# Batch 3's reciprocals sent through DMA, its last scores a group earlier: joining a pipeline's prologue to its steady pattern

## The chip, the cores and the metric

The kernel runs on 1 core of one Trainium2 chip. The metric is the device time in microseconds (us), where lower is better. Executions of the kernel before agree within about 0.3%, so runs are compared by the median and by a ratio. That ratio is the mean time of one kernel's fast runs over the mean time of the other's fast runs of the same rounds, with a 95% interval; it is not quite the quotient of the medians quoted here. The time before is 366.54 us. "Span" is the length of the one execution that the profiler recorded; it is a little shorter than the time (364.9 us for the kernel before).

## The reference

Eight batches of 576 tokens pass through sliding-window attention (window 128, a slope per head), and the 4608 tokens that come out pass through a gated FFN:

```python
scores = scale * np.matmul(q, k.transpose(0, 1, 3, 2))      # q, k, v: 8 x 8 heads x 576 x 64
scores = np.where(mask, scores + bias[None], -1000000000.0) # mask: 0 <= distance < 128
attn = np.exp(scores - max); attn = attn / attn.sum(axis=-1)
x = np.matmul(attn, v)                                      # then to (4608, 512)
out = (gelu(x @ w_gate) * (x @ w_val)) @ w_out              # 512 -> 1536 -> 512
```

## The kernel before

The FFN goes in nine groups of 512 tokens. Each group has an FFN part (12 gate/value blocks) and an output part (eight "halves", two for each tile of 128 tokens). The attention of later batches is woven between these, so that TensorE (PE) always has matmuls while ScalarE (ACT) does the exps and VectorE (DVE) the masks. A batch goes through five steps:

- q and k are transposed by DMA (`transposes_dma`, on the SP queue),
- scores, exps and mask (`scores2` for one block column, `scores` for the two parts s = 0, 1),
- row sums on PE and a reciprocal on DVE (`sums`),
- the spread of the reciprocals over all partitions, either by a small matmul (`spread_pe`) or through DRAM (`spread_dma`),
- values, multiplied by the spread reciprocal (`values`).

```python
def transposes_dma(b):                       # SP queue
    for src, dst in ((ks, kT), (qs, qT)):
        nc.sync.dma_start_transpose(out=dst[b % 2]..., in_=src[b % 2]...)

def spread_dma(b):                           # SP queue, behind whatever stands there
    d = d_pool.tile([4, 2, S], FP32, name="rd")
    nc.sync.dma_start(out=d..., in_=sumrow[b][0:128:16, :])           # rd <- r
    for i in (0, 1):
        nc.sync.dma_start(out=recip[b][64 * i:64 * i + 64, :, :],     # rb <- rd
                          in_=d[:, i, :].unsqueeze(0).to_broadcast((64, 4, S)))

def spread_pe(b, s):                         # four small matmuls into four banks
    ...                                      # and four copies on ACT and DVE
# ... cut ...
2: [("s", 3, 1, (0, 1), lambda: sums(3, 0)), 0, ("s", 3, 1, (2, 3)), 1,
    ("spread", 3, 0), ("pv", 3, 0), ("s2", 4), ("sum", 3, 1), 2,
    ("s", 4, 0, (0, 1)), 3, ("spread", 3, 1), ("pv", 3, 1), 4, ("s", 4, 0, (2, 3)), 5,
    ("s", 4, 1, (0, 1)), 6, 7, ("s", 4, 1, (2, 3))],
# ... cut ...
for g in range(NG):
    for b in ((), (2, 3), (4,))[g] if g < 3 else ():
        transposes_dma(b)
    if g + 2 < B:
        load_v(g + 2)                        # Pool queue: waits until vb's old batch is used up
    for f in range(3 if g == 0 else 0, NF):
        gate_val(g, f)
        # ... cut ...
        if 3 <= g < B - 1:                   # the steady pattern
            if f == 0:
                sums(g + 1, 0); sums(g + 1, 1)
                spread_dma(g + 1)
                if g + 2 < B:
                    transposes_dma(g + 2)
            elif f in (8, 10):
                for s in (0, 1):
                    values(g + 1, s, (f - 8, f - 7))
    if g + 3 < B:
        load_qk(g + 3)                       # Pool queue, behind load_v
    for item in steps(g):                    # output halves, scores and the rest, in order
        ...
```

The list for group 2 is written by hand: an integer is an output half, "s2" and "s" are scores, "sum" sums, "spread" the spread by PE, "pv" values. From group 3 on, every group has the same steady pattern.

The softmax here doesn't subtract the row's maximum and nothing guards it: scores larger than these inputs give would overflow.

## Time and profile before

| what | value |
|---|---|
| time, median of 3 | 366.54 us |
| profiled span | 364.9 us |
| PE busy | 351.6 us, 96% |
| share of PE in the chain that ended last | 86% |

The stretches view gives, for a window of time, the busy time of each engine (with the number of instructions in brackets), then the granted TensorE clock as a share of full speed, the DMA share and GB/s. For groups 2, 3 and 4 of the kernel before:

```profile
111.20:151.40 40.20, 39.73 (x325) 19.17 (x329) 24.55 (x39) 24.96 (x47) 17.81 (x23) 1.00 1.31 116
151.40:189.50 38.10, 37.41 (x285) 18.01 (x290) 22.18 (x33) 22.46 (x40) 16.62 (x20) 1.00 1.47 158
189.50:226.90 37.40, 37.14 (x285) 17.88 (x288) 20.88 (x32) 20.92 (x36) 4.19 (x5) 1.00 0.76 125
```

The third number is PE's busy time: it fills its group in all three, at full clock. Group 2 takes 40.2 us, group 3 38.1 and the fully steady group 4 37.4. So there is something to gain in groups 2 and 3, but only the few microseconds above 37.4, less the work that group 2 has beyond a steady group.

### The profile page before, as it was taken

The numbers are of one execution on the slowest core, as the hardware profiler recorded it, in microseconds if no ns is written. First come the engines' busy times: TensorE is split into PE (matmuls) and PEld (weight loads), VectorE is DVE, ScalarE is ACT, GpSimd is POOL, SyncE is SP. The second block draws the span as 40 slices with busy tenths as digits, with TensorE's granted clock in tenths as the row PEclk, the third lists the DMA queues.
The fourth block names the chain that finished last, engine by engine and source line by source line (L and its number), as shares of the span: only waits on it lengthen the run. The fifth ranks groups of instructions, "written<-read, shape, count | busy, mean of one in ns | idle before, by whom it ended". The sixth has DMA issues, their size and how long they took to land.

```text
span 364.9 us, 6652 instructions
## 1 busy us (share of the span) xinstructions
PE 351.6 (96%) x2638; PEld 170.7 (47%) x2682; DVE 189.0 (52%) x307; ACT 187.2 (51%) x339; POOL 108.1 (30%) x140
## 2 busy tenths in 40 slices
PE   8889999999999999999999999999999999999995
PEld 3455545444454445444444444444444444444442
DVE  4794448533795469474547554745564404302320
ACT  5953487435966376933783278436842223323321
POOL 8945859923519203900940040000000000000000
PEclk9999999999999999999999999999999999999999
DMA  9999999999999994999991992092206030011002
GB/s 105 133 202 180 171 160 183 178 152 194 140 150 98 147 105 81 147 106 224 116 202 53 224 91 89 32 216 58 88 31 131 0 115 2 0 60 58 0 31 86
DMA packets 151168, 41.41 MB, mean 113 GB/s; under 512 B 138816, under 2 KB 144448, under 8 KB 151136
## 3 DMA queue, kind: packets, MB, share of 16 engines
q0 software_dynamic: 112608, 18.88, 67.9%
q1 hardware_dynamic: 38528, 22.10, 28.4%
q8 instruction: 21, 0.34, 0.4%
q14 instruction: 11, 0.09, 0.1%
HBM read 42.47 MB, written 9.51 MB: 142 GB/s over the span
## 4 chain that ended last, share of the span: by engine, by line
PE 86%; ACT 8%; DVE 2%; issue 1%; POOL 1%; POOLq 0%; ACTq 0%; DVEq 0%
PE ps L292 50%; PE ps L308 23%; ACT P L181 6%; PE ps L273 4%; PE ps L174 4%; PE ps L232 2%; PE ps L255 1%; DVE xT L279 1%; DVE P L184 1%; ACT L181 1%; ACT emask L359 1%; PE ps L153 1%; DVE r L241 0%; POOL ks L115 0%; ACT osb L313 0%
## 5 line engine op out<-in xcount | busy, mean ns | idle before, releaser
L297 DVE TENSOR_TENSOR hT<-ps,gelu 128x512 bf16<-128x512 f32 (+2 forms) x111 | 74.4, 674 | 121.8 <-PE ps L292 107.1
L296 ACT ACTIVATE gelu<-ps 128x512 bf16<-128x512 f32 (+2 forms) x111 | 64.9, 586 | 120.0 <-PE ps L292 119.8
L292 PE MATMUL ps<-xT,wg 128*128 128x512 bf16 (+2 forms) x430 | 111.0, 373 | 1.7 <-DVE xT L279 0.7
L292 PE MATMUL ps<-xT,wv 128*128 128x512 bf16 (+2 forms) x435 | 110.4, 373 | 0.6
L308 PE MATMUL ps<-wo,hT 128*128 128x512 bf16 x413 | 97.2, 380 | 1.5 <-issue 0.8
L181 ACT ACTIVATE P<-ps 128x512 bf16<-128x512 f32 x144 | 74.3, 629 | 6.9 <-PE ps L174 6.8
L292 PEld LDWEIGHTS <-wv 128*128 128x128 bf16 x444 | 43.3, 98 | 50.5 <-issue 0.5
L292 PEld LDWEIGHTS <-wg 128*128 128x128 bf16 x444 | 41.9, 98 | 49.8 <-issue 2.3
L184 DVE TENSOR_TENSOR P<-P,emask 128x1024 bf16<-128x1024 bf16 x72 | 48.3, 685 | 31.2 <-ACT P L181 30.9
L308 PEld LDWEIGHTS <-hT 128*128 128x128 bf16 x432 | 39.7, 98 | 49.0 <-issue 4.4
L95 POOL DMA_DIRECT2D vb<-in_v_dram x40 | 33.7, 867 | 71.1 <-PE ps L273 70.4
L313 ACT COPY osb<-ps 128x512 f32<-128x512 f32 x36 | 21.7, 602 | 37.2 <-PE ps L308 32.8
L95 POOL DMA_DIRECT2D qs<-in_q_dram x35 | 29.7, 878 | 25.5 <-DMA qT<-qs 12.9
L95 POOL DMA_DIRECT2D ks<-in_k_dram x35 | 29.6, 882 | 9.6 <-DMA qs<-in_q_dram 6.6
L241 DVE RECIPROCAL r<-ps 128x320 f32<-128x320 f32 (+1 forms) x16 | 30.7, 1938 | 2.6 <-PE ps L232 2.6
L174 PE MATMUL ps<-qT,kT 64*128 64x256 bf16 (+1 forms) x384 | 23.5, 245 | 2.2 <-ACT kT L147 0.6
L279 DVE TENSOR_TENSOR xT<-ps,rb 128x320 bf16<-128x320 f32 (+1 forms) x64 | 24.7, 448 | 0.5 <-DMA rb<-rd 0.5
L174 PEld LDWEIGHTS <-kT 64*128 64x128 bf16 x384 | 12.9, 94 | 17.2 <-issue 12.7
L273 PE MATMUL ps<-P,vb 128*64 128x128 bf16 (+2 forms) x384 | 18.4, 243 | 0.1
L273 PEld LDWEIGHTS <-vb 128*64 128x64 bf16 x384 | 14.7, 110 | 6.8 <-issue 6.8
L232 PE MATMUL ps<-P,ones 128*32 128x128 bf16 (+2 forms) x384 | 10.8, 243 | 1.3 <-DVE P L184 1.1
L232 PEld LDWEIGHTS <-ones 128*32 128x32 bf16 x384 | 7.9, 96 | 5.5 <-issue 4.7
(50 smaller groups left out, 98.7 us busy)
## 6 DMA issues: line engine op xcount, KB each, us to landing
out_dram<-osb SPq DMA_DIRECT2D x36, 256.0 KB, 2.3
rb<-rd SPq DMA_DIRECT2D x8, 576.0 KB, 7.4
vb<-in_v_dram POOLq DMA_DIRECT2D x32, 128.0 KB, 5.7
qs<-in_q_dram POOLq DMA_DIRECT2D x28, 128.0 KB, 6.9
ks<-in_k_dram POOLq DMA_DIRECT2D x28, 128.0 KB, 6.3
wg<-in_moe_w_gate_dram POOLq DMA_DIRECT2D x4, 384.0 KB, 10.7
wv<-in_moe_w_val_dram POOLq DMA_DIRECT2D x4, 384.0 KB, 11.9
wo<-in_moe_w_out_dram POOLq DMA_DIRECT2D x2, 768.0 KB, 11.3
```

The lines of the kernel that those rows point to most:

```text
L95: nc.gpsimd.dma_start(out=t[lo:128, j, :].rearrange("p (h d) -> p h d", h=H), in_=src[b][:, 128 * j - 64 + lo:128 * j + 64, :].rearrange(" ...
L174: nc.tensor.matmul(out=ps[:, col:col + 128 * n].rearrange("p (n t) -> p n t", n=n), lhsT=blocks(kT, b, i, c, j, 1).rearrange("p n t -> p ( ...
L181: nc.scalar.activation(out=dst, in_=src, func=AF.Exp, scale=0.125)
L184: nc.vector.tensor_tensor(out=dst, in0=dst, in1=m, op=ALU.mult)
L232: nc.tensor.matmul(out=ps[32 * c:32 * c + 32, a:e], lhsT=ones[:, min(j, 1), i, :], rhs=prob(b, s, c, i, j, e - a), start=(i == 0 and j == ...
L241: nc.vector.reciprocal(sumrow[b][:, lo:hi], ps[:, 0:hi - lo])
L273: nc.tensor.matmul(out=ps[64 * i:64 * i + 64, a:e], lhsT=vb[b % 2][:, j, 64 * h:64 * h + 64], rhs=prob(b, s, c, i, j, e - a), start=(j == ...
L279: nc.vector.tensor_tensor(out=xT[:, c, b * S + lo:b * S + hi], in0=ps[:, 0:hi - lo], in1=recip[b][:, c, lo:hi], op=ALU.mult)
L292: nc.tensor.matmul(out=ps[:, 0:hi - lo], lhsT=w[:, c, 128 * f:128 * (f + 1)], rhs=xT[:, c, t0 + lo:t0 + hi], start=(c == 0), stop=(c == 3))
L296: nc.scalar.activation(out=gl[:, 0:hi - lo], in_=pg[:, 0:hi - lo], func=AF.Gelu)
L297: nc.vector.tensor_tensor(out=hid[g][:, f, lo:hi], in0=pv[:, 0:hi - lo], in1=gl[:, 0:hi - lo], op=ALU.mult)
L308: nc.tensor.matmul(out=po, lhsT=hid[g][:, f, 128 * t:128 * (t + 1)], rhs=wo[:, f, :], start=(f == 0), stop=(f == NF - 1))
```

## The change

The intent is to start the steady pattern one group earlier. The last scores of batch 3 move from group 2 to the end of group 1. Sums of batch 3 then come beside FFN blocks 0 and 1 of group 2; its reciprocals are spread through DMA and no longer by PE matmuls; its values come half at the 12th FFN block and half among the output halves. The transposes of batch 4, which stood first in group 2, now stand behind the spread on the SP queue, as they do in every steady group.

```diff
         1: [ ... cut ...
-            ("spread", 2, 1), ("pv", 2, 1), ("s", 3, 0, (2, 3)), 7],
-        2: [("s", 3, 1, (0, 1), lambda: sums(3, 0)), 0, ("s", 3, 1, (2, 3)), 1,
-            ("spread", 3, 0), ("pv", 3, 0), ("s2", 4), ("sum", 3, 1), 2,
-            ("s", 4, 0, (0, 1)), 3, ("spread", 3, 1), ("pv", 3, 1), 4, ("s", 4, 0, (2, 3)), 5,
-            ("s", 4, 1, (0, 1)), 6, 7, ("s", 4, 1, (2, 3))],
+            ("spread", 2, 1), ("pv", 2, 1), ("s", 3, 0, (2, 3)), 7, ("s", 3, 1, (0, 1)),
+            ("s", 3, 1, (2, 3))],
+        2: [("s2", 4), ("s", 4, 0, (0, 1)), 0, 1, ("s", 4, 0, (2, 3)), 2,
+            ("pv", 3, 0, (2, 3)), 3, ("s", 4, 1, (0, 1)), 4, ("pv", 3, 1, (2, 3)), 5,
+            ("s", 4, 1, (2, 3)), 6, 7],
# ... cut ...
-        for b in ((), (2, 3), (4,))[g] if g < 3 else ():
+        for b in ((), (2, 3))[g] if g < 2 else ():
             transposes_dma(b)
# ... cut ...
-            if 3 <= g < B - 1:
+            if 2 <= g < B - 1:
                 if f == 0:
                     sums(g + 1, 0)
+                if f == (1 if g == 2 else 0):
                     sums(g + 1, 1)
                     spread_dma(g + 1)
                     if g + 2 < B:
                         transposes_dma(g + 2)
-                elif f in (8, 10):
+                elif f in ((8, 10) if g > 2 else (11,)):
                     for s in (0, 1):
-                        values(g + 1, s, (f - 8, f - 7))
+                        values(g + 1, s, (0, 1) if f != 10 else (2, 3))
```

More of the change, by code (lines that the diff above doesn't have):

```diff
@@ L440 @@
     RUN = {"s2": scores2, "s": scores, "sum": sums, "spread": spread_pe,
-           "pv": lambda b, s: values(b, s, range(4))}
+           "pv": lambda b, s, cs=range(4): values(b, s, cs)}
     for g in range(NG):
-        for b in ((), (2, 3), (4,))[g] if g < 3 else ():
+        for b in ((), (2, 3))[g] if g < 2 else ():
             transposes_dma(b)
```

## The prediction

> **What bounds the kernel now.** I read the page first: the busy times, then the chain that ended last by engine.
>
> ```profile
> PE 351.6 (96%) x2638; PEld 170.7 (47%) x2682; DVE 189.0 (52%) x307; ACT 187.2 (51%) x339; POOL 108.1 (30%) x140
> PE 86%; ACT 8%; DVE 2%; issue 1%; POOL 1%; POOLq 0%; ACTq 0%; DVEq 0%
> ```
>
> TensorE (PE) is busy 96% of the 364.9 us span and carries 86% of the chain, so the time changes only by matmuls that leave PE and by gaps in which PE waits. Next I read the chain in order of time over groups 2 and 3, the stretch that the change touches.
>
> ```profile
> 131.97 0.61 PE ps L174 x12
> ...
> 136.54 0.75 PE ps L255 x8
> 137.29 1.11 PE ps L273 x24
> ...
> 142.63 0.66 PE ps L255 x8
> 143.29 1.00 PE ps L273 x24
> ...
> 150.88 0.56 PE ps L174 x12
> 151.45 2.08 ACT P L181 x4
> 153.55 0.70 DVE P L184
> 154.30 0.60 PE ps L232 x21
> ```
>
> L174 is scores, L232 sums, L255 the spread of the reciprocals by PE, L273 values, L292 gate and value products, L308 the output product. From the PE timeline, group 2 runs from 111.2 to 151.4 and group 3 from 151.45 to 189.5. Group 4, in full steady pattern, takes 189.52 to 226.91 = 37.4 us, group 3 takes 38.1: the last three lines of the fence show why. Its sums wait for the exps and the mask of scores issued at 150.88, the last thing of group 2. That is 0.65 us over a steady group.
>
> The third view is the timeline of the SP queue, which issues spread and transposes in one order. This is group 3:
>
> ```profile
> 159.86 0.71 SPq L245 DMA_DIRECT2D rd<-r  x1
> 161.74 1.32 SPq L247 DMA_DIRECT2D rb<-rd  x2
> 163.29 6.85 SPq L167 DMA_TRANSPOSE kT<-ks  x1
> 170.31 3.10 SPq L167 DMA_TRANSPOSE qT<-qs  x1
> ```
>
> and this, in the DMA view of 170 to 176 us, is the last of them, with the time from issue to landing at the end:
>
> ```profile
> qT<-qs SPq DMA_TRANSPOSE x1, 4.9
> ```
>
> So from the end of the last reciprocal (159.83 on the DVE timeline) to q transposed in place is 170.31 + 4.9 - 159.83 = 15.4 us. The same sum gives 206.50 + 6.5 - 196.5 = 16.5 in group 4 and 244.09 + 5.3 - 233.9 = 15.5 in group 5. The scores that read it start at 176.26, 213.72 and 251.12, only 1.1, 0.7 and 1.7 us after the landings. The steady pattern hides this DMA chain, but with almost nothing to spare.
>
> **What the Trainium skill says.** "TensorE: Matmul & The Clock Gate", Part 3 (The mechanism): matmuls at different row groups of the array overlap. The trace agrees: the eight instructions of a spread take 0.66 to 0.75 us together, although one of them lasts 453 ns on average. So removing a spread is worth far less than its busy durations suggest. "DMA: Bandwidth & Descriptors", Anatomy of one DMA: about 2 us of a transfer is fixed, mostly completion. The trace agrees: 1.88 us pass between issuing the 18 KB rd and issuing rb, which waits for it. "ScalarE: Activation LUTs", What ACT_TABLE_LOAD costs: 1283 ns of load plus a drain, 2.66 us together. The trace shows the 1.28 us load and the next gelu 0.01 us behind it (112.26 and 113.55), so I count 1.28. The first page's Part 1: an idle PE falls to half clock after about a 3.4 us window; here the granted clock is 1.00 from 361 to 364 us and 0.57 from 364 to 365, so it falls at about 364.1, some 3 us after the last matmul ended at 361.1.
>
> **The change, part by part.**
>
> *Removed.* Both spreads of batch 3: 0.75 + 0.66 = 1.41 us of PE, all on the chain. Some 0.3 us of issue gaps between the many pieces of group 2 may go as well (the chain has 0.15 us at 131.82 and 0.16 us at 135.14). Four ACT and four DVE copies of about 0.44 us leave too, off the chain.
>
> *Moved out of group 3's way.* Group 2 now ends like a steady group, with two output tiles after the last scores. So the mask wait at the head of group 3 goes: -0.65 us.
>
> *Moved without cost of their own.* Sums (1.05 us, 48 matmuls) and values of batch 3 only change place. The last scores of batch 3 (24 matmuls, 1.09 us) go from group 2 to the end of group 1.
>
> *The new end of group 1.* Now two score calls follow output tile 7 with nothing between. I worked through ACT: exps of the earlier scores end at 111.76, the copy of tile 7 at 112.24 (both as now), then eight exps take 4.03 us (the run of eight at 133.12) to 116.15, the table load to 117.43, the first gelu to 118.05. PSUM has eight banks in rotation: the second half of the last score call needs tile 7's bank, free at 112.24, and the first gate product needs the bank of the first new exp, free at about 112.75. PE would reach that point at 112.3 (111.2 + 1.09), so it loses about 0.45 us. Group 2 starts at 112.78.
>
> *The reciprocals.* DVE takes them in program order: first product by 118.7, reciprocal 0 (about 2.1 us) by 120.8, second product by 121.4, reciprocal 1 (1.7) by 123.05. In steady groups the second reciprocal ends 7.0 us after the group starts (196.5 - 189.52); here it is 10.3, because ACT is behind and the second sum waits until gate block 1.
>
> *The DMA chain.* The reciprocals now go through rd and rb, and the transposes of batch 4 stand behind them on SP. Before, these were issued at 112.83, free of any reciprocal. Last reciprocal at 123.05 + 15.5 us (median of the three) = 138.55 until q of batch 4 is transposed.
>
> *Who needs it.* The first score call of batch 4 is now the very first item after the FFN of group 2. PE reaches it at 112.78 + 1.73 (gate 0) + 0.53 (sums) + 1.73 (gate 1) + 0.53 (sums) + 17.27 (ten gates of 1.727) + 0.1 (issue) + 1.06 (values beside block 11) = 135.7. **It waits 138.55 - 135.7 = 2.85 us.**
>
> *The sum.* Scores start at 138.6. A steady group needs 213.72 to 226.91 = 13.2 us from there, plus the two half values, 1.06 us: group 3 starts at about 152.9, against 151.45 now, +1.45. Group 3 then saves 0.65. Net +0.8 us; groups 4 to 8 repeat the same pattern. 366.54 + 0.8 = 367.3. I choose **367.4** because what is uncertain lies more on the slow side.
>
> **Rivals.**
>
> *The wait doesn't appear.* For it: the q and k loads of batch 5 (Pool, 112.08 to 125.1, slowed now by the transposes of batch 4) would run uncontended, and a wait needs 2.85 us of my arithmetic to hold. Against it: all three steady instances take over 15 us, and only 12.65 us lie between reciprocal and use. Without the wait the time is 366.54 - 1.41 - 0.3 - 0.65 + 0.45 = about 364.6.
>
> *The DMA chain is slower than in steady groups.* When transposes and loads ran together now, k and q took from 112.83 to 126.79 to issue, 14.0 us, against 10.1 us in group 3. If the loads of batch 5 overlap rd and rb by some us, the wait grows to 4 us, and the time to about 368.5. For it: DMA is at 9 tenths in this stretch. Against it: with the transposes away, the loads should be over near 125.7, by the run of loads issued back to back from 147 to 155.4.
>
> *The clock falls.* A gap near 3 us is where the clock fell at the end of the run. If it falls in the wait, the next 3.4 us run at half speed: about +1.7 us, to 369. I give it 1 in 5.
>
> *A later echo.* Values of batch 3 end some 4 us later than now, and the loads of v 5 and of q and k 6 wait for them; they would run into rb of group 3, where the slack was 1.1 us. The reciprocals there come no sooner, so I expect under 0.5 us.
>
> *ACT becomes the bound at the start of group 2.* It is 4 us behind, but eight banks let PE run on: the banks that gates 3 to 6 need come free at 118.7, 120.8, 121.5 and 123.9, which is before PE asks, except at gate 4, where the two are about even.
>
> **Range and chances.** From "no wait" (364.6) to "wait with a fallen clock" (369 to 370); the middle eight tenths are 365.2 to 369.6. A 2% step is 7.3 us: a gain of that size would need five times the work removed, a loss would need a wait of 9 us. Faster 0.01, within 0.97, slower 0.02.
>
> **What would show it.** In the changed trace: no L255 instruction after about 109; a gap of about 0.45 us on PE just before group 2; the rd issue at about 123; a PE gap of 2 to 4 us before L174 at 136 to 139, put down to a transpose (it may be named otherwise, since its releaser is a DMA); sums at the head of group 3 without a wait; group 3 in 37.4 us. It is wrong if q of batch 4 lands before 136, if the reciprocals end by 120, or if PE stalls at gates 3 to 6 for banks.

## The result, and the profile after

The changed kernel takes 371.48 us (370.96 to 372.10, 4 runs), where the kernel before took 366.65 us in the same rounds. The ratio to the kernel before is 1.0132, interval 1.0114 to 1.0149: 1.3% slower, where 0.2% was predicted, and above the predicted range. Executions over 1.5% slower than the fastest of the same kernel are left out of the means. The profiled span is 369.4 us against 364.9.

The page of the changed kernel, the lines that answer to those shown of before, and the row of the granted clock (40 slices of the span, in tenths):

```profile
PE 353.0 (96%) x2622; PEld 170.8 (46%) x2666; DVE 187.5 (51%) x303; ACT 186.0 (50%) x335; POOL 108.0 (29%) x140
PEclk9999999999999996999999999999999999999999
PE 84%; ACT 7%; DMA 3%; DVE 2%; issue 2%; POOL 1%; SPq 0%; POOLq 0%; ACTq 0%; DVEq 0%
```

By its records PE has 16 matmuls fewer, yet is busy 1.4 us longer. DMA appears in the chain with 3%, which it did not before. And in one slice the clock is down.

The stretches of groups 2, 3 and 4 of the changed kernel:

```profile
112.60:156.24 43.64, 40.10 (x283) 18.72 (x288) 23.17 (x35) 23.78 (x43) 13.61 (x18) 0.92 1.04 123
156.24:194.20 37.96, 37.31 (x284) 18.02 (x289) 21.04 (x32) 20.92 (x36) 19.25 (x23) 1.00 1.65 169
194.20:231.60 37.40, 37.14 (x285) 17.88 (x288) 20.89 (x32) 20.92 (x36) 4.18 (x5) 1.00 0.74 123
```

Group 3 starts at 156.24 in place of 151.4, 4.8 us later. Of these, 1.4 us lie at the end of group 1, where the moved scores now stand, and 3.4 us in group 2, although that group holds less work. Group 3 itself gains only 0.14 us. From group 4 on all is as before. So the loss that has to be explained lies in group 2, and the first place to look is its SP queue (start, time on the queue, line, kind, names). Before, the transposes of batch 4 stood alone there:

```profile
112.83 6.05 SPq L167 DMA_TRANSPOSE kT<-ks  x1
119.05 7.74 SPq L167 DMA_TRANSPOSE qT<-qs  x1
```

In the changed kernel they stand behind the spread:

```profile
122.97 0.71 SPq L245 DMA_DIRECT2D rd<-r  x1
124.98 1.32 SPq L247 DMA_DIRECT2D rb<-rd  x2
126.53 7.33 SPq L167 DMA_TRANSPOSE kT<-ks  x1
134.03 3.35 SPq L167 DMA_TRANSPOSE qT<-qs  x1
```

The same stretch in the chain in order of time, and then on PE, where the bracket at the end of a line is the idle time before it and what ended it:

```profile
134.03 4.86 DMA qT<-qs
138.89 0.14 issue
139.02 1.47 PE ps L174 x16
```

```profile
134.85 1.13 PE L273 MATMUL ps<-P,vb 128*64 128x192 bf16 x24
139.02 1.47 PE L174 MATMUL ps<-qT,kT 64*128 64x128 bf16 x16 [3.04 <-DMA qT<-qs]
140.42 0.61 PE L308 MATMUL ps<-wo,hT 128*128 128x512 bf16 x1
141.25 4.08 PE L308 MATMUL ps<-wo,hT 128*128 128x512 bf16 x10 [0.22 <-issue]
```

The last reciprocal ends at 122.9, rd is issued at once, q of batch 4 lands at 138.89, and PE has nothing to do from 135.98 to 139.02. This is the predicted wait. What follows it is the surprise: 16 score matmuls take 1.47 us where a steady group has 0.77, and ten output matmuls 4.08 us where twelve of a steady group take 2.70. The stretches view of the changed kernel shows why:

```profile
136.00:138.00 2.00, 0.00 (x0) 0.00 (x0) 1.18 (x4) 0.00 (x0) 0.00 (x0) 0.99 1.24 269
138.00:139.00 1.00, 0.00 (x0) 0.01 (x1) 0.00 (x0) 0.00 (x0) 0.00 (x0) 0.50 0.37 70
143.00:145.00 2.00, 2.00 (x7) 0.72 (x5) 0.41 (x1) 0.00 (x0) 0.00 (x0) 0.55 0.00 0
145.00:147.00 2.00, 2.00 (x16) 0.81 (x14) 0.03 (x1) 1.64 (x4) 0.00 (x0) 1.00 0.09 34
```

The clock goes to half at 138 and comes back at 144.8; the clock record of the trace has 137.96 and 6.83 us. Of these, 5.77 us lie after the restart at 139.02, so the slow clock costs half of that, 2.9 us.

### The profile page after: what moved, and what is told of

It is laid out like the page before. It is cut to its first block, busy times and chain, and to the rows that moved or that the text cites. A ratio compares the mean times of both kernels' runs of the same rounds, so it can differ in the third digit from the quotient of the medians.

```text
span 369.4 us, 6613 instructions
## 1 busy us (share of the span) xinstructions
PE 353.0 (96%) x2622; PEld 170.8 (46%) x2666; DVE 187.5 (51%) x303; ACT 186.0 (50%) x335; POOL 108.0 (29%) x140
## 4 chain that ended last, share of the span: by engine, by line
PE 84%; ACT 7%; DMA 3%; DVE 2%; issue 2%; POOL 1%; SPq 0%; POOLq 0%; ACTq 0%; DVEq 0%
PE ps L292 49%; PE ps L308 23%; ACT P L181 5%; PE ps L174 4%; PE ps L273 3%; DMA qT<-qs 3%; PE ps L232 2%; DVE xT L279 1%; PE ps L255 1%; ACT L181 1%; ACT emask L359 1%; DVE P L184 1%; PE ps L70 1%; PE ps L153 1%; DVE r L241 0%
## 5 line engine op out<-in xcount | busy, mean ns | idle before, releaser
L308 PE MATMUL ps<-wo,hT 128*128 128x512 bf16 x414 | 99.3, 385 | 1.5 <-issue 0.9
L174 PEld LDWEIGHTS <-kT 64*128 64x128 bf16 x384 | 13.4, 96 | 19.5 <-issue 15.3
## 6 DMA issues: line engine op xcount, KB each, us to landing
wo<-in_moe_w_out_dram POOLq DMA_DIRECT2D x2, 768.0 KB, 10.1
```

Of the source, the lines that this page charges most:

```text
L174: nc.tensor.matmul(out=ps[:, col:col + 128 * n].rearrange("p (n t) -> p n t", n=n), lhsT=blocks(kT, b, i, c, j, 1).rearrange("p n t -> p ( ...
L308: nc.tensor.matmul(out=po, lhsT=hid[g][:, f, 128 * t:128 * (t + 1)], rhs=wo[:, f, :], start=(f == 0), stop=(f == NF - 1))
```

## The experiments

The theory is: (a) PE waits because the transposes of batch 4 stand behind the reciprocals and the spread on one queue; (b) the wait makes the clock fall, which costs nearly as much again; (c) the late values of batch 3 delay loads, which then slow the spread of group 3, an echo. The rivals are that the new places of the scores, sums and values cost by themselves, or that ACT, 4 us behind at the start of group 2, is the bound. All outputs are right. Each ratio and each time before is of the same rounds, on one chip; runs of different experiments can come from different chips.

### 1. One part alone: the moved scores

```diff
 kernel before
-  ("spread", 2, 1), ("pv", 2, 1), ("s", 3, 0, (2, 3)), 7],
-  2: [("s", 3, 1, (0, 1), lambda: sums(3, 0)), 0, ("s", 3, 1, (2, 3)), 1,
+  ("spread", 2, 1), ("pv", 2, 1), ("s", 3, 0, (2, 3)), 7, ("s", 3, 1, (0, 1)), ("s", 3, 1, (2, 3))],
+  2: [("sum", 3, 0), 0, 1,
```

> The kernel before with one part of the change alone: the last scores of batch 3 move to the end of group 1, the spread stays on PE and the transposes stay first. Theory (this part costs only the short waits for ACT at the end of group 1, about 0.45 us, less the issue gaps that it removes): 366.65 + 0.2, within 0.6 us of the kernel before. Rival (ACT, 4 us behind at the start of group 2, is what made the changed kernel slow): over 369.

Measured: 367.95 us against 367.25, ratio 1.0019 (1.0002 to 1.0035): 0.7 us slower, a little more than the 0.6 us allowed for. The rival falls: the back-to-back scores and the ACT that is behind cost under 1 us.

### 2. One part undone: the transposes first

```diff
 changed kernel
-    for b in ((), (2, 3))[g] if g < 2 else ():
+    for b in ((), (2, 3), (4,))[g] if g < 3 else ():
         transposes_dma(b)
@@ behind spread_dma(g + 1)
-                    if g + 2 < B:
+                    if 4 < g + 2 < B:
                         transposes_dma(g + 2)
```

> The changed kernel with one part undone: the transposes of batch 4 issued at the start of group 2, ahead of the spread of batch 3, as before. Theory (PE waits because the transposes stand behind the reciprocals on the SP queue): q of batch 4 lands by about 128, the gap before its first scores and the clock fall are gone, time about 371.5 - 3.0 - 2.8 = 365.7 or a little less, though rd can't be issued before about 127 and the values of batch 3 may then wait for rb until 137. Rival (the new end of group 1 with its back-to-back scores costs the time, or the values at block 11): the time stays within 1 us of 371.5.

Measured: 374.32 us against 367.25, ratio 1.0188 (1.0149 to 1.0226). It is slower still, so my expectation was wrong. Its SP queue, and the line of DVE that multiplies the first values:

```profile
118.90 7.96 SPq L167 DMA_TRANSPOSE qT<-qs  x1
126.95 0.71 SPq L245 DMA_DIRECT2D rd<-r  x1
133.56 1.31 SPq L247 DMA_DIRECT2D rb<-rd  x2
```

```profile
141.33 1.55 DVE L279 TENSOR_TENSOR xT<-ps,rb 128x320 bf16<-128x320 f32 x4 [5.61 <-DMA rb<-rd]
```

Now q is in place in time and rb is late. The 18 KB of rd, issued behind the transposes while the loads of batch 5 also run, take 6.6 us from issue to the issue of rb, which waits for them (126.95 to 133.56), against 2.0 us in the changed kernel. DVE waits 5.61 us for rb, PE's banks stay full, and PE waits 5.34 us. The clock, which was expected to stay, falls in this wait too (3.41 us from 141.69 on). So the order on the queue is not the cause alone: the spread and the transposes together, with the loads around them, are too long for the order of work that this version has behind the FFN, and undoing the order on the queue only chooses which of the two is late. The Trainium skill has a possible reason why a small transfer can take so long, "DMA: Bandwidth & Descriptors", Queues, rings and completion order: each DMA engine takes the queue rows it has work for in turn, a whole packet at a time. The 6.6 us agree with that, but no run here shows single turns.

### 3. The whole DMA chain undone: the spread back on PE

```diff
 changed kernel, with the transposes first as in 2
-                    spread_dma(g + 1)
-                    if g + 2 < B:
-                        transposes_dma(g + 2)
+                    if g > 2:
+                        spread_dma(g + 1)
+                        if g + 2 < B:
+                            transposes_dma(g + 2)
+                elif g == 2 and f in (5, 6):
+                    spread_pe(3, f - 5)
```

> The changed kernel with the spread of batch 3 back on PE (beside FFN blocks 5 and 6) and the transposes of batch 4 first again, so no reciprocal goes through DMA in group 2; scores, sums, values and the order of the rest stay as changed. Theory (all of the loss is the DMA chain rd, rb, transposes, and the clock fall it causes): no gap before the first scores of batch 4, no clock fall, 1.41 us of spread matmuls back, ratio to the kernel before about 1.000 and a spread between runs under 1 us. Rival (the new places of scores, sums and values cost by themselves): ratio over 1.006.

Measured: 368.13 us against 366.75, ratio 1.0027 (1.0009 to 1.0046). In group 2 the gap and the clock fall are gone. But the ratio is not 1.000, the runs spread over 2.0 us, and the profile has a wait in a place where I had not expected one of this size, at the first scores of group 3:

```profile
159.74 0.71 SPq L245 DMA_DIRECT2D rd<-r  x1
163.48 1.32 SPq L247 DMA_DIRECT2D rb<-rd  x2
```

```profile
178.63 0.83 PE L174 MATMUL ps<-qT,kT 64*128 64x128 bf16 x16 [1.70 <-DMA qT<-qs]
```

rd to rb takes 3.74 us here against 1.88 in group 3 of the kernel before. This is the echo, and it is the subject of the next two runs.

### 4. The echo taken away

```diff
 changed kernel (loads_swapped), and the kernel of 3 (pe_back_swapped)
+        if g == 3:
+            load_qk(6)
         if g + 2 < B:
             load_v(g + 2)
@@ after the FFN part
-        if g + 3 < B:
+        if g != 3 and g + 3 < B:
             load_qk(g + 3)
```

The load of v of batch 5 overwrites the buffer of batch 3, so it waits for the last values of batch 3. In the changed kernel that is 151.94 us (its second part on the Pool queue), where it was 144.43. The loads of q and k of batch 6 stand behind it.

> The changed kernel with the loads of q and k of batch 6 queued ahead of the load of v of batch 5, so that they need not wait for the values of batch 3 and are over before group 3's reciprocals. Theory of an echo (these loads run into rd and rb of group 3): in group 3 the time from issuing rd to issuing rb falls from 3.97 to about 1.9 us, the wait of DVE for rb (1.69 us) and of PE for q of batch 5 (0.34) go, time 0.3 to 0.6 us lower, about 371. The wait in group 2 stays at 3 us. Rival (rd is slow in group 3 for another reason): 3.97 stays.

> The version with the spread of batch 3 back on PE, with the loads of q, k 6 queued ahead of the load of v 5 as well. In that version group 3 took 39.15 us against 37.4 of a steady group, and rd to rb 3.74 us. Theory (the echo, late loads that run into rd and rb of group 3, is worth 1.75 us there): rd to rb falls to about 1.9 us, group 3 to 37.4, span from 367.3 to about 365.5, ratio about 0.998. Rival (group 3 is slow there for another reason): ratio stays at 1.003.

Measured: pe_back_swapped 367.10 us against 367.18, ratio 0.9999 (0.9983 to 1.0015), and four runs within 0.5 us. rd to rb is 1.87 us:

```profile
159.79 0.71 SPq L245 DMA_DIRECT2D rd<-r  x1
161.66 1.32 SPq L247 DMA_DIRECT2D rb<-rd  x2
```

Group 3 takes 37.4 us in it, against 39.15. The span goes from 367.3 to 365.6, so the echo was 1.7 us in the profiled execution of that version. In times the difference is smaller and not clear: the ratios, 1.0027 and 0.9999, are of two chips, and their intervals overlap. This run also gave the 1.000 that run 3 had been expected to give.

loads_swapped: 371.37 us against 366.75, ratio 1.0120 (1.0099 to 1.0142). Its rd to rb in group 3 fell from 3.97 to 1.81 us, and its group 3 from 37.96 to 37.4 us, as expected. In the changed kernel the echo is thus worth 0.55 us in the profiled execution. In times, its ratio can't be told apart from the 1.0132 of the changed kernel. Its four times go with the granted clock: 369.95 us at 0.999, 370.76 at 0.995, 371.98 and 372.11 at 0.991.

### 5. The clock kept up in the wait

```diff
 changed kernel
-        2: [("s2", 4), ("s", 4, 0, (0, 1)), ...
+        2: [("busy", 12), ("s2", 4), ("s", 4, 0, (0, 1)), ...    # warm6: 6 in place of 12
@@
-    RUN = {"s2": scores2, ...
+    RUN = {"busy": keep_busy, "s2": scores2, ...
```

`keep_busy(n)` is the kernel's own helper: the next bank first receives n matmuls of zeros, which the scores then overwrite.

> The changed kernel with twelve matmuls of zeros (0.22 us each, 2.6 us) put into the wait before the first scores of batch 4, where PE stood idle 3.04 us and the granted clock then fell to 0.50 from about 138 to 145. Theory (the wait itself costs 3.0 us and the clock fall it causes another 2.8): the landing of q of batch 4 stays at 138.9 us, the clock stays at 1.00, the rest of group 2 takes 14.3 us in place of 17.3, time about 371.5 - 2.8 = 368.7. Rival (the loss after the wait comes from the new order of products and values itself, the clock is only a sign of it): time stays at 371.5 or rises.

> The changed kernel with six zero matmuls (1.3 us) at the start of its wait, half of those of the earlier run: they shorten the idle stretch from 3.0 to about 1.7 us but do not fill it. Theory (the clock falls after about 2 to 3 us of idle PE, whatever else is in the order): no fall, clock 0.999 to 1.000, the wait ends when it did, same time as with twelve, ratio about 1.006. Rival (only a filled gap keeps the clock): clock 0.991 to 0.995, ratio as the changed kernel. A third outcome, both levels in different runs, would mean that the fall depends on where a free-running window stands.

> A repeat of the run with twelve zero matmuls, whose four times spread over 4.8 us (368.51 to 373.29) although three of them had a clock of 1.000. Theory (the DMA chain's own length varies from run to run): median 1.5 to 3 us below the unaltered changed kernel of the same chip, spread again over 1.5 us. Rival (the first set was disturbed): four times within 0.7 us, ratio about 1.006.

> The changed kernel unaltered, on the same chip as the two runs with zero matmuls, as their base. Expected: ratio to the kernel before 1.011 to 1.015, granted clock 0.991 or 0.995 in nearly every run.

| run | median | four times | ratio (interval) |
|---|---|---|---|
| warm12 | 370.06 | 368.51, 370.93, 373.29, 369.19 | 1.0091 (1.0038 to 1.0144) |
| after_again | 370.64 | 370.71, 375.55, 369.84, 370.56 | 1.0083 (1.0056 to 1.0109) |
| warm6 | 369.83 | 369.17, 372.16, 368.67, 370.49 | 1.0080 (1.0039 to 1.0122) |
| warm12_again | 370.00 | 370.64, 368.51, 372.62, 369.35 | 1.0085 (1.0038 to 1.0132) |

The 375.55 of after_again does not enter its ratio; the median of its three fast runs is 370.56 us. That ratio, 1.0083, lies below the 1.011 to 1.015 that were expected, and its interval does not meet that of the same kernel's first measurement (1.0114 to 1.0149). So the ratio of one kernel can differ by 0.5% from one set of rounds to another, and ratios of different sets can't be compared more closely than that.

In the profiled executions the theory holds: in none of the three warm runs does the clock fall near the wait, and from the first scores of batch 4 to group 3 the chain has 14.65 us in each of them, against 17.4 in the changed kernel and 16.3 in after_again, whose fall lasts 3.41 us. For warm6 this is shown for that one execution only. Its four granted clocks are 0.994, 0.995, 1.000 and 0.995, not the 0.999 to 1.000 that were expected; the 0.994 is a fall at 11.34 us, in the start-up, and where the falls of the two runs at 0.995 lie is not known.

And the times don't show the gain. Medians of warm runs and of the unaltered kernel lie within 1 us, and the expected 1.5 to 3 us are missing. The profile of warm12_again shows one reason, again at the first scores of group 3:

```profile
180.41 0.84 PE L174 MATMUL ps<-qT,kT 64*128 64x128 bf16 x16 [1.89 <-DMA qT<-qs]
```

Here the echo costs 1.9 us, while the profiled executions of warm12 and warm6 have no wait at that place. So the echo differs from one execution to the next, and it can hide the clock. That called for one more pair, in which the echo is taken out of both.

### 6. The clock alone

The edit of warm12 on loads_swapped, beside loads_swapped itself, five rounds each on the same chip.

> The changed kernel without the echo in group 3, as base for the next run on the same chip. Expected: ratio to the kernel before near 1.012, runs at the granted clocks 0.991, 0.995 or 0.999, slower the lower the clock.

> The changed kernel with twelve zero matmuls in its wait and without the echo in group 3 (loads of q, k 6 ahead of v 5): the clock fall alone is taken from loads_swapped_again. Theory (the fall costs 1.7 or 2.85 us in each execution, and only the echo, 0 to 2 us, hid this in the times of the earlier runs): times lie 1.5 to 3 us below loads_swapped_again, within 1 us of each other, near 368.7, ratio about 1.005. Rival (the fall costs little in executions that aren't profiled): both ratios within 0.002.

Measured: loads_swapped_again 370.77 us, ratio 1.0100 (1.0080 to 1.0120), granted clock 0.995 in five runs and 0.991 in one. warm12_swapped 368.69 us, ratio 1.0044 (1.0031 to 1.0057), clock 0.998 to 1.000, six runs within 0.5 us. The two intervals don't touch. The first scores of batch 4 in the two profiles, loads_swapped_again first:

```profile
140.83 1.47 PE L174 MATMUL ps<-qT,kT 64*128 64x128 bf16 x16 [3.46 <-DMA qT<-qs]
139.88 0.84 PE L174 MATMUL ps<-qT,kT 64*128 64x128 bf16 x16 [0.64 <-DMA qT<-qs]
```

With the wait filled, 2.1 us of time are gone, and with the echo gone too, so is the wide scatter of the warm runs. Not all of the 2.1 us can be put down to the clock: a granted clock of 0.995, which five of the six runs of loads_swapped_again have, amounts to one fall of 3.41 us, and such a fall costs at most half of that, 1.7 us; in the two profiles the chain from these scores to group 3 goes from 16.1 to 14.65 us, 1.45 us. The remaining 0.4 us or more are not explained.

### 7. The dose of the wait

```diff
 changed kernel
-                if f == (1 if g == 2 else 0):
+                if f == (4 if g == 2 else 0):
                     sums(g + 1, 1)
```

> The changed kernel with the second sums, and so the whole DMA chain behind them, at FFN block 4 in place of 1: the last reciprocal ends some 2.7 us later (at about 125.6). Theory (the wait is set one to one by the end of the last reciprocal plus the chain): q of batch 4 lands about 2.7 us later, the gap grows from 3.0 to 5.7 us, the clock fall stays one fall, time about 371.5 + 2.7 = 374.2. Rival (the chain is held up by something else, such as the loads of batch 5, so that the start hardly matters): landing and time within 0.8 us of the changed kernel's.

Measured: 372.06 us (median of its three fast runs; the fourth, 377.11, is slow) against 366.75, ratio 1.0136 (1.0121 to 1.0152). The last reciprocal ends 2.0 us later (124.95 against 122.95), not the 2.7 I had worked out. q lands 1.3 us later, and the gap is longer:

```profile
140.37 0.83 PE L174 MATMUL ps<-qT,kT 64*128 64x128 bf16 x16 [4.18 <-DMA qT<-qs]
```

So the wait follows the reciprocals, though not one to one, for the chain behind them took 15.3 us in place of 15.9. The time did not follow, and the 374.2 us that were expected did not come: in the profiled execution the clock fall lasted 3.41 us and not 6.83, which gives back about what the longer wait took. Where the clock falls has to be read before a time is put down to a wait.

### 8. Two orders that cover the wait

```diff
 values_first: changed kernel, only the list of group 2
-        2: [("s2", 4), ("s", 4, 0, (0, 1)), 0, 1, ("s", 4, 0, (2, 3)), 2,
-            ("pv", 3, 0, (2, 3)), 3, ("s", 4, 1, (0, 1)), 4, ("pv", 3, 1, (2, 3)), 5,
-            ("s", 4, 1, (2, 3)), 6, 7],
+        2: [0, ("pv", 3, 0, (2, 3)), 1, ("pv", 3, 1, (2, 3)), ("s2", 4), ("s", 4, 0, (0, 1)),
+            2, ("s", 4, 0, (2, 3)), 3, 4, ("s", 4, 1, (0, 1)), 5, ("s", 4, 1, (2, 3)), 6, 7],
```

```diff
 transposes_between: changed kernel
-        2: [("s2", 4), ("s", 4, 0, (0, 1)), 0, 1, ... ]
+        2: [0, ("s2", 4), ("s", 4, 0, (0, 1)), 1, ("s", 4, 0, (2, 3)), 2,
+            ("pv", 3, 0), 3, ("pv", 3, 1), ("s", 4, 1, (0, 1)), 4, 5, ("s", 4, 1, (2, 3)), 6, 7],
@@ in spread_dma, between the issue of rd and that of rb, for batch 3 only
+        transposes_dma(4)
@@ the values beside FFN block 11 are dropped
```

> The changed kernel with only the order of the work after the FFN of group 2 changed: two output tiles' halves and both remaining value blocks of batch 3 come ahead of the first scores of batch 4, some 3.8 us of PE work. Theory (a wait of 3.04 us for q of batch 4, and its clock fall): the wait is covered, the clock stays, and the loads of v 5 and q, k 6 start about 9 us sooner, so group 3 has no echo either: about 364.6 us, below both kernels. Rival (transposes are merely hidden elsewhere, the rest costs as much): 366 to 371.

> A version meant to beat both: as changed, but on the SP queue the transposes of batch 4 go between rd and rb, one output half precedes the first scores of batch 4, and all values of batch 3 come after output halves 2 and 3, when rb has landed. Theory: q of batch 4 lands at about 136, just when PE asks (136.3), rb by about 142, before the values need it at 143; no wait over 0.5 us, clock stays, time about 2.5 us below the kernel before, ratio 0.993 to 0.996. Rival (rb behind the transposes comes too late): PE or DVE waits for rb by 1 us or more, ratio about 1.00.

values_first: 366.02 us against 367.25, ratio 0.9971 (0.9956 to 0.9985). transposes_between: 365.48 us against 366.75, ratio 0.9968 (0.9956 to 0.9981). Both beat both kernels, though by less than was expected (364.6 us, and a ratio of 0.993 to 0.996). In values_first PE does two halves and two value blocks while q is on its way, and the wait is down to 0.21 us:

```profile
139.45 0.63 PE L273 MATMUL ps<-P,vb 128*64 128x128 bf16 x12
140.29 0.84 PE L174 MATMUL ps<-qT,kT 64*128 64x128 bf16 x16 [0.21 <-DMA qT<-qs]
```

Because batch 3's values end sooner, the loads behind them start sooner, and its group 3 is a steady one:

```profile
112.70:151.30 38.60, 38.18 (x289) 17.93 (x289) 22.94 (x34) 23.52 (x43) 20.33 (x25) 1.00 1.55 157
151.30:188.70 37.40, 37.40 (x290) 17.88 (x288) 21.46 (x32) 20.98 (x37) 12.56 (x15) 1.00 1.28 152
```

In transposes_between, q is no longer awaited, and rb, issued at 131.33, is there before the values ask for it. The two versions are not separable from each other.

## Why the prediction was right or wrong

**What held.** The start of group 2 was worked out as 112.78 and is 112.67. The last reciprocal was put at 123.05 and ends at 122.95. The DMA chain was put at 15.5 us and took 15.9. PE was to reach the first scores of batch 4 at 135.7, and reached them at 136.0. The wait was to be 2.85 us and is 3.04; that it came so close is in part luck, for both of its ends came 0.3 us late. PE does not stall for banks at gates 3 to 6. Each of these was read off steady groups of the kernel before, and each held within half a microsecond.

**The step that failed is the clock.** The prediction had the fall as a rival, "I give it 1 in 5", with "about +1.7 us", and left it out of the predicted sum. The granted clock is 0.991 or 0.995 in all four runs of the changed kernel, and in all six profiles in which PE waits 3.0 us or more in group 2 (3.04 to 5.34) the clock falls in that wait, so it was not a chance of one in five. In the three profiles with a wait of 1.7 to 1.9 us it does not fall there. In the profiled execution of the changed kernel the fall lasted two windows of 3.41 us and not one, and cost 2.9 us. In times, it is worth up to 2.1 us by the pair of experiment 6. With the predicted 366.54 + 0.8 and this term the time would have been 369.4 to 370.2, so this is the largest part of the miss.

**The echo was mis-sized as well.** The prediction expected under 0.5 us from the late loads, and a group 3 that saves 0.65. In the profile group 3 saves 0.14: the mask wait at its head is gone, as predicted, but 0.55 us is given back. In other executions it can be more; 1.7 and 1.9 us were seen in two of the experiments' profiles.

**The sum in the profile.** Group 3 was to start at 152.9 and starts at 156.28. The difference of 3.4 us is 0.4 from the landing of q (139.02 for 138.6) and 3.0 from the stretch behind it (17.26 for 14.25), of which 2.9 is the clock. With the 0.5 that group 3 lacks, this gives the 3.9 us between the predicted loss of 0.8 and what the groups show, 4.83 - 0.14 = 4.7.

**The rival "the wait doesn't appear"** had 364.6 us. The two orders that cover the wait come to 0.997 of the kernel before, 1.1 to 1.2 us below it and not 1.9. What holds back the rest is not settled: in values_first the first exps wait for an output copy that stands ahead of them on ACT, and 0.21 us of the wait are left, but I did not take these away one at a time.

**What stays open.** loads_swapped_again has runs at the same granted clock of 0.995 that lie 1.8 us apart (369.50 to 371.31). The profile shows one execution only, so how the length of the wait varies between executions, and how much of the fall is spent while PE is idle anyway, is argued and not shown. Nor is it known why the changed kernel came to 1.0132 in its first rounds and to 1.0083 in after_again; a fall of two windows in two of the first four runs (0.991), and of one in the fast runs of the second set (0.995), can be part of it.

## What to carry to other kernels

A steady pattern hides a chain of transfers only by the time that lies between its start and its use; when it is moved to a group where the start comes later, read that distance again (here 16 to 17 us became 13 for a chain of 15 to 16) and put other work in between. A wait of PE of 3 us or more was priced twice here, once as the wait and once as the slow clock after it, so count the second term as likely and not as a rival. And when a buffer is set free later, follow the load that waits for it: it ran into the next group's small transfers, and cost up to 1.9 us far from the change.

## What the Trainium skill lacked or had wrong

- "TensorE: Matmul & The Clock Gate", Part 1, gives an idle window of about 3.4 us before the clock halves, free-running. The falls here do last one or two windows (3.41 and 6.83 us), but no idle stretch of a whole window is needed: the changed kernel's PE was idle for 1.98 us when its clock fell (135.98 to 137.96). The window that ends with that fall, 3.41 us long, had PE busy for its first 1.43 us, 42%. Windows with 47% (warm6, from 137.64), 49% (transposes_first, from 134.86) and 52% (sums_late, from 134.41) ended without a fall. This makes no rule, for in the start-up of warm6 a window with 65% (from 7.93) ended with one. Once at half, the clock stayed there for a second window when PE was busy in 63% of the first (changed kernel) or 77% (loads_swapped), and came back after one with 84% (loads_swapped_again).
- "ScalarE: Activation LUTs", What ACT_TABLE_LOAD costs, adds a drain of 1380 ns to the load of 1283. In the kernel before, the load starts 0.02 us after the copy ahead of it ends (112.24 and 112.26), and the next gelu 0.01 us after the 1.28 us load ends.
- "DMA: Bandwidth & Descriptors" has about 2 us fixed for a transfer, in a section on DMAs issued from GpSimd. For rd, issued on SP, that held in a quiet stretch (1.81 to 1.88 us from issuing rd to issuing rb in group 3), but it has no figure for a small transfer beside others: the same 18 KB took 3.6 to 4.2 us beside the loads of q and k, and 6.6 us behind transposes and beside loads.
- No page gives the time of a DMA transpose from SBUF to SBUF in the presence of loads. Issuing k and q of a batch (128 x 2560 each) took 10.1 us in group 3 of the kernel before and 14.0 us in its group 2, beside the loads of batch 5.
